# A mean in two parts and a product group in another place: a recurrent attention kernel with a SoLU layer

## The chip, the cores and the metric

The kernel runs on one core of a Trainium2 chip. The metric is the device time of one execution in microseconds (us), as the median of several runs. The core has five engines with their own instruction queues: TensorE (PE in the profile; its weight loads are PEld), VectorE (DVE), ScalarE (ACT), GpSimd (POOL) and SyncE (SP). Matrix products go to PSUM, and the other engines take them from there. DMAs are issued from the queues of SP, POOL and ACT.

## The reference

Two layers follow one another. The first is a recurrence over 768 steps for each of 4 x 8 heads with a state of 40 x 40. The second is a feed-forward layer with a softmax-weighted activation (SoLU) and a layer norm before the output product:

```python
for t in range(S):
    y[:, :, t] = np.einsum('bhd,bhde->bhe', rt, state)
    Sa = np.einsum('bhde,bhe->bhd', state, at)
    state_decay = state * wt[:, :, None, :] - np.einsum('bhd,bhe->bhde', Sa, bt)
    state = state_decay + np.einsum('bhd,bhe->bhde', vt, kt)
...
h = x @ w_in                                  # 3072 x 320 @ 320 x 1024
e = np.exp(h - np.max(h, axis=-1, keepdims=True))
solu = h * (e / (np.sum(e, axis=-1, keepdims=True) + 1e-09))
mu = np.mean(solu, axis=-1, keepdims=True)
var = np.mean((solu - mu) ** 2, axis=-1, keepdims=True)
return ((solu - mu) / np.sqrt(var + 1e-06) * g_ln) @ w_out
```

All inputs of the recurrence are float32. The weights `w_in` and `w_out` reach the kernel as 64-bit words, which it turns into float32 itself.

## The kernel before

The recurrence is done in chunks of 64 steps. Two of the four batches and all eight heads of one chunk make one unit of work, numbered `i` from 0 to 23. For each unit a triangular system is inverted, and the chunk's output and new state come out of products of 64 x 64 or 40 x 64 blocks, each of which uses a quarter of TensorE's array. The feed-forward layer takes the 128 finished rows of a unit some rounds later with products over the full array.

One main loop, `for i in range(-1, N + 3 + LAG)`, interleaves the stages of several units. A round `i` finishes unit `i`, prepares unit `i+1`, begins unit `j = i + 5`, and does the feed-forward layer for unit `m - 2 = i - 3` and its output for unit `m - 3 = i - 4`. The order of the instructions on PE, POOL, DVE and SP is the order in which the program text issues them; each of these engines works through its queue in that order. ScalarE's order is set by a planner. Synchronization follows from the tiles that instructions read and write, and from the buffers that tiles share.

The pieces that matter here, in the order of a round:

- `some(n)` issues n steps of the inversion (`prod` L404 and `uu` L406 on VectorE). `narrow` turns weights from 64-bit words to float32, on VectorE and ScalarE (L182 to L195), with some of those steps between. The eight chunks `c` of `w_out` (128 rows each) go to `w2[:, c]`; the sixth is turned at the end of round 2, the seventh and eighth in round 3.
- `carried` and `driven` (`px`), then `front(j)`: transposes of `a` and `b` of unit j (`pa`, `pb`); VectorE makes `aT` (L347) out of the first, ScalarE copies the second to `bT`. Then half of a feed-forward product, `hidden` (`h`).
- `solved` (`pu`), `attend_kv(i+1)` (transposes of k and v: `pk`, `pv`, copied by ScalarE to `kT`, `vT`), again `hidden`, `attend_rs(i+1)` (transposes of r and of the state: `pr`, `pst`), the rest of `hidden`, and `exped` (`nmax` L644 and `e` L647).
- `decay_turned` (`pei`, copied by ScalarE to `ex` L339), `scaled(j+1)` (two products on POOL, `kb` L318), `left(i-1)` (six DMAs on POOL, `xT<-x`).
- `answered` (`pl`, and VectorE's mask of it to `lu`), `norm(j)` (16 products `pnt` of bT and aT, VectorE's mask of them to `nt` L351, and a DMA of `nt` on POOL's queue L377), `flip` (`tu` L431), `weighed` and `spreadof`, `decay` (`pcum`).
- In round 4 (`i == 3 + LAG`) `centre_w2`: eight products `pmean` (L221) give the mean of the rows of `w2`, and one VectorE instruction (L222) subtracts it from all of `w2`. This takes the layer norm's mean out of the output product.
- `output(m-3, 0)` (`po` L692, first four of eight products with `w2`), `scores` (`ps`), `couple` (`py`), `output(m-3, 1)` (the rest of `po`, then `osb`), `close` (`pz`), `read` (`pyo`), `leave` (`x` L593), `folded` (`plnT`, copied to `lnT`). The first output is that of round 4.

A float32 product is issued as two passes, so the eight products of `pmean` are 16 instructions in the profile.

PSUM is divided among three pools: `banks` (two slots of two banks), `h` (one slot of two banks), and `bank` (two slots of one bank). `pa`, `pb`, `pk`, `pv`, `pr`, `pst`, `pei`, `pcum`, `pmean`, `po` and `plnT` share the two slots of `bank`; `px`, `pu`, `pl`, `pnt`, `ps`, `py`, `pz`, `pyo` share those of `banks`. A tile waits until the one that held its slot has been read.

Of the kernel before, what the change touches and what calls it, by code (L numbers as in the profile page):

```python
# [9 lines left out]
FP32 = mybir.dt.float32  # L10
# [4 lines left out]
ALU = mybir.AluOpType  # L15
PSUM = bass.MemoryType.PSUM
AX = mybir.AxisListType
P = 128
# [6 lines left out]
LAG = 1  # L25
# [23 lines left out]
def kernel(  # L49
# [18 lines left out]
    nc = tc.nc  # L68
    B, H, S, D = r.shape
    DM = H * D  # L70
# [4 lines left out]
    NF = DFF // P  # L75
# [5 lines left out]
    two = ctx.enter_context(tc.tile_pool(name="two", bufs=2))  # L81
# [14 lines left out]
    def c_(name):  # L96
        lo, hi = where[name]
        return cst[:, lo:hi]

    ident, tri = c_("ident"), c_("tri")  # L100
# [18 lines left out]
    for x in ex_t:  # L119
# [10 lines left out]
                          in_=c_("eye_hi").unsqueeze(1).to_broadcast([P, 8, Q]))  # L130
    w_in = const.tile([P, 2 * NK - 1, DFF // 2], FP32, name="w_in")
    w2 = const.tile([P, NF, DM], FP32, name="w2")
# [3 lines left out]
    def banks(name):  # L136
        return ps1.tile([P, 2, 512], FP32, tag="banks", name=name)

    def bank(name):
        return ps3.tile([P, 512], FP32, tag="bank", name=name)  # L140
# [74 lines left out]
        for x, y in zip(g_cols, (0, -20, -36)):  # L215
            nc.scalar.mul(out=x, in_=pg[:, 0:NF], mul=2.0 ** y)

    def centre_w2():
        t = bank("pmean")
        for c in range(NF):  # L220
            nc.tensor.matmul(t[:, 0:DM], lhsT=c_("mean"), rhs=w2[:, c, :], start=c == 0, stop=c == NF - 1)  # L221
        nc.vector.tensor_tensor(out=w2, in0=w2, in1=t[:, 0:DM].unsqueeze(1).to_broadcast([P, NF, DM]),  # L222
                                op=ALU.subtract)


    def half(p):
        return slice(C * p, C * p + C)
# [6 lines left out]
    def in_turn(tile_of, some=units):  # L234

        lots = {}
        for u in some:
            lots.setdefault(tile_of(*u), []).append(u)
        lots = list(lots.values())
        return [lot[n] for n in range(max(map(len, lots))) for lot in lots if n < len(lot)]  # L240

    def mm(o, lhsT, rhs, start=True, stop=True):
        nc.tensor.matmul(o, lhsT=lhsT, rhs=rhs, start=start, stop=stop, skip_group_check=True)  # L243
# [15 lines left out]
    def where_(i):  # L259
        return i % NPAIR, i // NPAIR  # L260

    def load(x, ap, i, queue=nc.sync):
        bp, ci = where_(i)
        for p in range(2):
            queue.dma_start(out=x[half(p), :, 0:D],  # L265
                              in_=ap[2 * bp + p, :, ci * C:(ci + 1) * C, :].rearrange("h t d -> t h d"))

    def ok(i):
        return 0 <= i < N


    def load_keys(i, names, queue=nc.sync):
        if not ok(i):
            return
        for n, ap in (("w", w), ("b", b), ("a", a), ("k", k)):
            if n in names:
                x = a_t[i % 4] if n == "a" else two.tile([P, H, D], FP32, tag="raw_" + n, name="raw_" + n,
                                                             bufs=3)
                st[i]["raw_" + n] = x
                load(x, ap, i, queue)  # L280
# [39 lines left out]
    def turned(name, x):  # L320
        t = bank("p" + name)
        for j in range(4):
            nc.tensor.transpose(out=t[0:W2, j * P:(j + 1) * P],  # L323
                                in_=x[:, 2 * j:2 * j + 2].rearrange("p a b -> p (a b)")[:, 0:W2], identity=ident)
        return t[0:W2].rearrange("p (j b t) -> p b j t", j=4, b=2)

    def tokens(name, bufs=1):
        return two.tile([P, 2, 4, C], FP32, tag=name, name=name, bufs=bufs)

    def kept(name, t, bufs=1):  # L330
        o = tokens(name, bufs)
        nc.scalar.copy(out=o[0:W2], in_=t)
        return o
# [16 lines left out]
    def masked(dst, t):  # L350
        nc.vector.tensor_tensor(out=dst, in0=t.rearrange("p b (j c) -> p b j c", j=4),  # L351
                                in1=tri.unsqueeze(1).unsqueeze(1).to_broadcast([P, 2, 4, C]), op=ALU.mult)

    def keyed(t, u):
        p, q, g, h = u
        return t[rows(h), p, 2 * q + g]
# [5 lines left out]
    def norm(i):  # L362
        if not ok(i):
            return
        d = st[i]
        t = banks("pnt")
        for u in in_turn(lambda p, q, g, h: (h, p ^ h)):
            p, q, g, h = u
            j = 2 * q + g
            mm(t[half(p ^ h), h, j * C:j * C + C], keyed(d["bT"], u), keyed(d["aT"], u))  # L370
        nt = d["nt"] = tokens("nt", AHEAD)
        masked(nt, t[:, :, 0:256])
        n, at = divmod(i, GRP)
        if at == 0:
            blocks[n] = dram.tile([2 * GRP * H, C, C], FP32, tag="nt_dram", name="nt_dram")
        queue = nc.sync if i < 4 else nc.gpsimd
        queue.dma_start(out=blocks[n].rearrange("(a h x) s c -> a x s h c", a=GRP, x=2)[at].rearrange("x s h c -> (x s) h c"),  # L377
                          in_=nt.rearrange("p h j c -> p (h j) c"))
# [36 lines left out]
    def bring(i):  # L415
        if not ok(i):
            return
        d = st[i]
        d["tu"], d["uh"] = tu_t[i % 2], uh_t[i % 2]
        n, at = divmod(i, GRP)  # L420
        src = inverse[n].rearrange("(e a h x) c t -> e a h x c t", e=2, a=GRP, x=2)
        for x in range(2):
            nc.sync.dma_start(out=d["tu"][C * x:C * x + Q, :, Q:2 * Q], in_=src[0, at, :, x].rearrange("h c t -> c h t"))
        for x in range(2):
            nc.sync.dma_start(out=d["uh"][C * x + Q:C * x + C], in_=src[1, at].rearrange("h x c t -> c (h x) t"))
# [40 lines left out]
    def attend_rs(i):  # L466
        if not ok(i):
            return
        d = st[i]
        bp, ci = where_(i)  # L470
        d["rT"] = kept("rT", turned("r", r_t[0]), 2)
        if ci:
            t = bank("pst")
            for x in range(4):
                nc.tensor.transpose(out=t[0:W2, x * P:(x + 1) * P],
                                    in_=st_t[bp][:, 2 * x:2 * x + 2].rearrange("p a b -> p (a b)")[:, 0:W2], identity=ident)
            d["s"] = two.tile([P, 4, P], FP32, tag="s", name="s")
            nc.scalar.copy(out=d["s"][0:W2], in_=t[0:W2].rearrange("p (x t) -> p x t", x=4))
# [148 lines left out]
    def hidden(i, some):  # L627

        if not ok(i):
            return  # L630
        d = st[i]
        for kt, x in some:
            if (kt, x) == (0, 0):
                d["h"] = ps2.tile([P, DFF], FP32, tag="h", name="h")
            part = slice(0, P) if kt < 2 else half(x)
            mm(d["h"][:, 512 * x:512 * x + 512], d["xT"][part, kt], w_in[part, 2 * kt + (x if kt < 2 else 0)],
               start=kt == 0, stop=kt == NK - 1)
# [64 lines left out]
    def some(n):  # L702
        while steps and n:
            if next(steps[0], steps) is steps:
                steps.pop(0)
            else:
                n -= 1
# [3 lines left out]
    def begin_inverse(n):  # L711
        steps.append(invert(n))
        next(steps[-1])
# [60 lines left out]
    for i in range(-1, N + 3 + LAG):  # L774
        j, m = i + AHEAD, i - LAG
        pieces = shares.get(i, (3, 6, 0, 6))
        some_weights = narrowed.get(i, (0, 0))

        some(pieces[0])
        if i >= 1:  # L780
            bring(i + 1)
        if i >= 0:
            load_values(i + 2)
        carried(i)
        driven(i)
        front(j)
        hidden(m - 2, ((0, 1),))
        load_keys(j + 3, "w")
        load_keys(j + 2, "bak")
        narrow(some_weights[0], pieces[1])  # L790

        solved(i)
        attend_kv(i + 1)
        hidden(m - 2, ((1, 1),))
        attend_rs(i + 1)
        hidden(m - 2, ((2, 0), (2, 1)))
        exped(m - 2)
        decay_turned(j + 1)
        scaled(j + 1)
        left(i - 1)  # L800

        answered(i)
        norm(j)
        if i >= 0:
            flip(i + 1)
        weighed(m - 2)
        spreadof(m - 2)
        decay(j + 2)
        if i == 0:
            turn_g()  # L810
        if i == 3 + LAG:
            centre_w2()
        output(m - 3, 0)
        if ok(j) and j % GRP == GRP - 1:
            begin_inverse(j // GRP)
        some(pieces[2])
        scores(i + 1)
        if i < 0:
            flip(i + 1)
        couple(i + 1)  # L820
        output(m - 3, 1)
        narrow(some_weights[1], pieces[3])

        close(i + 1)
        read(i, True)
        read(i, False)
        by_value(i + 2)
        leave(i)
        folded(m - 2)
        hidden(m - 1, ((0, 0), (1, 0)))  # L830
# [30 lines left out]
```

## Time and profile before

| | |
|---|---|
| median of 3 runs | 643.66 us (641.3 to 646.32) |
| the profiled execution: whole time | 642.36 us |
| its span | 640.3 us |
| mean granted clock of TensorE | 0.924 |
| PE busy | 565.3 us |
| DVE busy | 483.0 us |
| POOL busy | 269.1 us |
| ACT busy | 245.1 us |

A busy share is an average over stages with different limits. The span and the 2.1 us around it make the whole time of that one execution. Waits are read where they stand: "[3.00 <-DVE w L222]" behind an instruction says that its engine stood for 3.00 us and that the VectorE instruction of line 222, which writes `w`, ended it. In a line of the timeline the first number is the start in us from the begin of the span, the second the length in us; "x16" is the number of instructions that are merged in the line.

### The profile page before, as it was taken

How to read it: one execution, taken by the hardware profiler on the slowest of the kernel's cores; microseconds unless marked ns; L12 is line 12 of the kernel's file. 1: busy time of each engine (PE TensorE's matmuls, PEld its weight loads, DVE VectorE, ACT ScalarE, POOL GpSimd, SP SyncE). 2: the span in 40 equal slices, each digit the busy share in tenths (PEclk: the TensorE clock that was granted, in tenths of full speed). 3: DMA queues.
4: the chain of work that ended last, by engine and by line, in shares of the span. 5: the costliest groups of instructions: out<-in, count | busy, mean ns of one | idle time of the engine just before them, and what ended most of it. 6: DMA issues, size and time to landing. Idle time of an engine off the chain costs nothing.

```text
span 640.3 us, 26725 instructions
## 1 busy us (share of the span) xinstructions
PE 565.3 (88%) x11449; PEld 400.6 (63%) x11449; DVE 483.0 (75%) x1285; ACT 245.1 (38%) x497; POOL 269.1 (42%) x444
## 2 busy tenths in 40 slices
PE   4246597788889999999999999999999999999995
PEld 3124476656556767777667767776776676766653
DVE  4577798889858988878979889888887797433431
ACT  4313445553404334424433443443334333332221
POOL 3333355671524544472573545454624632322200
PEclk9665668797889999999999999999999999999998
DMA  8949896663426355454544554563523422210000
GB/s 165 161 76 161 166 170 129 136 138 70 89 53 112 79 112 111 85 111 92 111 98 96 108 101 99 108 124 74 109 52 70 101 45 50 51 37 26 24 20 20
DMA packets 217868, 59.92 MB, mean 94 GB/s; under 512 B 203216, under 2 KB 213048, under 8 KB 217752
## 3 DMA queue, kind: packets, MB, share of 16 engines
q1 hardware_dynamic: 200984, 34.47, 31.8%
q0 software_dynamic: 11376, 19.25, 12.5%
q10 hardware_dynamic: 5392, 4.51, 2.5%
q8 instruction: 90, 1.47, 1.0%
q14 instruction: 26, 0.21, 0.1%
HBM read 40.10 MB, written 13.37 MB: 84 GB/s over the span
## 4 chain that ended last, share of the span: by engine, by line
PE 70%; DVE 15%; DMA 7%; issue 3%; ACT 3%; SPq 1%; ACTq 0%; DVEq 0%; POOL 0%; POOLq 0%
PE po L692 16%; PE h L243 14%; PE pyo L243 7%; DVE prod L404 4%; PE pu L243 3%; PE px L243 3%; DVE uu L406 3%; PE ps L243 3%; DMA xT<-x 3%; PE plnT L681 2%; PE pl L243 2%; PE pz L243 2%; PE pei L323 2%; PE pk L323 2%; PE pr L323 2%
## 5 line engine op out<-in xcount | busy, mean ns | idle before, releaser
L404 DVE TENSOR_TENSOR prod<-blk,uu 128x30 f32<-128x30 f32 (+4 forms) x360 | 120.2, 334 | 16.4 <-DMA blk<-nt_dram 6.3
L243 PE MATMUL h<-w_in,xT 128*128 128x512 f32 (+1 forms) x288 | 122.0, 617 | 0.0
L692 PE MATMUL po<-w,lnT 128*128 128x320 f32 x384 | 115.2, 445 | 3.0 <-DVE w L222 3.0
L406 DVE TENSOR_TENSOR uu<-uu,prod 128x30 f32<-128x30 f32 (+4 forms) x360 | 105.7, 294 | 12.4
L692 PEld LDWEIGHTS po<-w,lnT 128*128 128x128 f32 x384 | 71.3, 192 | 33.2 <-issue 6.7
L644 DVE TENSOR_REDUCE nmax<-h 128x1 f32<-128x1024 f32 x24 | 29.4, 1224 | 56.4 <-PE h L243 56.4
L670 POOL TENSOR_TENSOR rs<-c,mhalf 128x1 f32<-128x1 f32 x24 | 13.4, 558 | 108.4 <-DVE c L669 108.4
L377 POOL DMA_DIRECT2D nt_dram<-nt x20 | 18.6, 929 | 89.1 <-DVE nt L351 76.3
L612 POOL TENSOR_TENSOR st<-tot,ex 104x160 f32<-104x160 f32 x44 | 22.2, 521 | 78.9 <-DVE tot L608 78.2
L243 PEld LDWEIGHTS h<-w_in,xT 128*128 128x128 f32 (+1 forms) x288 | 39.0, 191 | 21.7 <-issue 18.8
L624 POOL DMA_DIRECT2D xT<-x x96 | 48.7, 513 | 0.0
L682 ACT COPY lnT<-plnT 128x512 f32<-128x512 f32 x48 | 26.1, 588 | 43.6 <-PE plnT L681 39.9
L388 POOL DMA_DIRECT2D blk<-nt_dram x42 | 33.3, 798 | 18.0 <-DMA nt_dram<-nt 17.7
L243 PE MATMUL pyo<-lv,kb 64*64 64x104 f32 x768 | 37.9, 269 | 2.7
L647 ACT ACTIVATE e<-h,nmax 128x1024 f32<-128x1024 f32 x24 | 26.7, 1114 | 29.5 <-DVE nmax L644 28.5
L243 PE MATMUL pyo<-lu,kb 64*64 64x104 f32 x768 | 36.6, 262 | 0.0
L265 POOL DMA_DIRECT2D raw_r<-in_r_dram x48 | 35.0, 733 | 0.0
L653 DVE TENSOR_TENSOR e<-h,e 128x1024 f32<-128x1024 f32 x24 | 28.8, 1198 | 5.8 <-ACT e L647 5.8
L661 DVE BATCH_NORM_STATS2 bs<-e 128x6 f32<-128x512 f32 x48 | 30.9, 685 | 0.8
L443 ACT ACTIVATE wy<-py,cst 128x256 f32<-128x256 f32 x24 | 11.3, 472 | 52.4 <-PE py L243 52.4
L696 ACT ACTIVATE osb<-po,rs 128x320 f32<-128x320 f32 x24 | 12.7, 527 | 48.6 <-PE po L692 29.7
L318 POOL TENSOR_TENSOR kb<-raw_k,inv 128x320 f32<-128x320 f32 x24 | 21.6, 901 | 20.5 <-DMA raw_k<-in_k_dram 20.5
(125 smaller groups left out, 1133.8 us busy)
## 6 DMA issues: line engine op xcount, KB each, us to landing
blk<-nt_dram POOLq DMA_DIRECT2D x42, 128.0 KB, 3.7
nt_dram<-nt POOLq DMA_DIRECT2D x20, 256.0 KB, 4.0
raw_w<-in_w_dram SPq DMA_DIRECT2D x48, 80.0 KB
a<-in_a_dram SPq DMA_DIRECT2D x48, 80.0 KB
raw_r<-in_r_dram POOLq DMA_DIRECT2D x48, 80.0 KB, 3.3
lv<-in_v_dram SPq DMA_DIRECT2D x48, 80.0 KB
out_dram<-osb ACTq DMA_DIRECT2D x24, 160.0 KB
raw_b<-in_b_dram SPq DMA_DIRECT2D x44, 80.0 KB
```

The costliest lines, as they stand in the source:

```text
L243: nc.tensor.matmul(o, lhsT=lhsT, rhs=rhs, start=start, stop=stop, skip_group_check=True)
L265: queue.dma_start(out=x[half(p), :, 0:D], in_=ap[2 * bp + p, :, ci * C:(ci + 1) * C, :].rearrange("h t d -> t h d"))
L323: nc.tensor.transpose(out=t[0:W2, j * P:(j + 1) * P], in_=x[:, 2 * j:2 * j + 2].rearrange("p a b -> p (a b)")[:, 0:W2], identity=ident)
L388: queue.dma_start(out=nb[home:home + Q], in_=blocks[n][:, Q * e:Q * e + Q, Q * e:Q * e + Q])
L404: nc.vector.tensor_tensor(out=t, in0=nb[:, j:j + 1, j + 1:Q].to_broadcast([P, n_c, m]), in1=u[:, 0:n_c, j:j + 1].to_broadcast([P, n_c, m]) ...
L406: nc.vector.tensor_tensor(out=u[:, 0:n_c, j + 1:Q], in0=u[:, 0:n_c, j + 1:Q], in1=t, op=ALU.subtract)
L624: nc.gpsimd.dma_start(out=xT[to:to + Q, 2], in_=x[at + P - 3 * D:at + D, 2])
L644: nc.vector.tensor_reduce(out=nmax, in_=d["h"], axis=AX.X, op=ALU.max, negate=True)
L647: nc.scalar.activation(out=e, in_=d["h"], func=AF.Exp, bias=nmax, accum_out=d["esum"])
L653: nc.vector.tensor_tensor(out=d["e"], in0=d["h"], in1=d["e"], op=ALU.mult)
L661: nc.vector.bn_stats(out=bs[:, x], in_=d["e"][:, x * 512:x * 512 + 512])
L692: nc.tensor.matmul(d["out"][:, 0:DM], lhsT=d["lnT"][:, f, :], rhs=w2[:, f, :], start=f == 0, stop=f == NF - 1)
```

## The change

`centre_w2` is split in two functions. `mean_begun(6)` runs in round 3 (`i == 2 + LAG`), at the place in the round where `centre_w2` stood in round 4: it adds up the first six chunks in a `bank` slot and ScalarE copies the sum to an SBUF tile, which uses the buffer of `osb`. `centred(mean, 6)` runs in round 4 after the first `hidden` and ahead of `narrow` and `solved`: a product with the identity puts the sum back into a `bank` slot, two products add the last two chunks, and VectorE subtracts the mean from `w2` in two instructions of half the size. `norm(j)` moves in every round from behind `answered` to between `hidden(m-2, ((1, 1),))` and `attend_rs`.

```diff
-    def centre_w2():
+
+    def mean_begun(n):
         t = bank("pmean")
-        for c in range(NF):
-            nc.tensor.matmul(t[:, 0:DM], lhsT=c_("mean"), rhs=w2[:, c, :], start=c == 0, stop=c == NF - 1)
-        nc.vector.tensor_tensor(out=w2, in0=w2, in1=t[:, 0:DM].unsqueeze(1).to_broadcast([P, NF, DM]),
-                                op=ALU.subtract)
+        for c in range(n):
+            nc.tensor.matmul(t[:, 0:DM], lhsT=c_("mean"), rhs=w2[:, c, :], start=c == 0, stop=c == n - 1)
+        mean = two.tile([P, DM], FP32, tag="osb", name="mean", bufs=1)
+        nc.scalar.copy(out=mean, in_=t[:, 0:DM])
+        return mean
+
+    def centred(mean, n):
+        t = bank("pmean")
+        nc.tensor.matmul(t[:, 0:DM], lhsT=ident, rhs=mean, start=True, stop=False)
+        for c in range(n, NF):
+            nc.tensor.matmul(t[:, 0:DM], lhsT=c_("mean"), rhs=w2[:, c, :], start=False, stop=c == NF - 1)
+        for x in range(0, NF, NF // 2):
+            nc.vector.tensor_tensor(out=w2[:, x:x + NF // 2], in0=w2[:, x:x + NF // 2],
+                                    in1=t[:, 0:DM].unsqueeze(1).to_broadcast([P, NF // 2, DM]), op=ALU.subtract)
...
         driven(i)
         front(j)
         hidden(m - 2, ((0, 1),))
+        if i == 3 + LAG:
+            centred(mean, 6)
         load_keys(j + 3, "w")
...
         solved(i)
         attend_kv(i + 1)
         hidden(m - 2, ((1, 1),))
+        norm(j)
         attend_rs(i + 1)
...
         answered(i)
-        norm(j)
...
-        if i == 3 + LAG:
-            centre_w2()
+        if i == 2 + LAG:
+            mean = mean_begun(6)
         output(m - 3, 0)
```

## The prediction

> **What bounds the kernel now.** First the page's bars of 40 slices and the totals:
>
> ```profile
> PE 565.3 (88%) x11449; PEld 400.6 (63%) x11449; DVE 483.0 (75%) x1285; ACT 245.1 (38%) x497; POOL 269.1 (42%) x444
> ...
> PE   4246597788889999999999999999999999999995
> ...
> PEclk9665668797889999999999999999999999999998
> ```
>
> From the thirteenth slice on TensorE is at 9 and its clock is full; before that neither is. So there are two stages. The table of windows puts numbers on rounds of the main loop (`i`; a round starts with `px`):
>
> ```profile
> 217.40:239.60 22.20, 21.98 (x498) 15.69 (x493) 19.46 (x51) 9.23 (x19) 12.79 (x21) 1.00 0.55 110
> ...
> 171.00:181.20 10.20, 7.40 (x90) 4.76 (x86) 8.54 (x12) 2.70 (x6) 4.08 (x6) 1.00 0.41 88
> 181.20:184.60 3.40, 3.20 (x6) 2.19 (x7) 0.06 (x1) 0.00 (x0) 1.40 (x3) 0.50 0.32 86
> ```
>
> Columns: window, its length, then busy us of PE, PEld, DVE, ACT, POOL, granted clock, DMA share, GB/s. Round 6 (217.4) has PE busy 21.98 of 22.2 us; DVE has nearly 3 us to spare. From round 5 on, whatever PE must do more is paid in full. The other two windows lie in round 4, where the change works. Its timeline:
>
> ```profile
> 164.44 0.83 DVE L406 TENSOR_TENSOR uu<-uu,prod 128x126 f32<-128x126 f32 x1
> ...
> 165.81 0.68 DVE L347 TENSOR_TENSOR aT<-pa,ex 104x512 f32<-104x512 f32 x1
> ...
> 166.65 0.62 PE L323 MATMUL pv<-cst,v 128*104 128x128 f32 x4 [2.43 <-DVE aT L347]
> ...
> 173.93 4.47 PE L221 MATMUL pmean<-w,cst 128*128 128x320 f32 x16
> ...
> 178.44 2.82 DVE L222 TENSOR_TENSOR w<-w,pmean 128x2560 f32<-128x2560 f32 x1 [0.76 <-PE pmean L221]
> ...
> 181.40 3.98 PE L692 MATMUL po<-w,lnT 128*128 128x320 f32 x8 [3.00 <-DVE w L222]
> ...
> 185.32 0.69 PE L243 MATMUL ps<-aT,kT 40*64 40x64 f32 x32
> ```
>
> PE computes the mean (16 passes, 0.27 us apart), stands 3.00 us for the subtraction, and then runs `po` at half clock. `pv`, earlier, stood 2.43 us for `aT`: a wait on VectorE. For rounds 0 to 3, the waits between 60 and 195 us:
>
> ```profile
> PE pr L323 <- ACT kT L332: 6.0, 3, 2.2
> ...
> DVE lu L351 <- PE pl L243: 2.0, 2, 1.1
> ```
>
> PE waits about 2 us a round before `pr` (line: total, times, longest). The chain of waits runs through VectorE there (`prod`, `uu` and `w` steps), so a PE gap filled is worth only what VectorE gets from it: its two waits of about 1 us for `pl`.
>
> Last, a saturated round (10), for what the order of PE's groups costs:
>
> ```profile
> 308.06 1.02 PE L243 MATMUL h<-w_in,xT 128*128 128x512 f32 x2
> 309.01 0.69 PE L243 MATMUL pu<-tu,x 64*64 64x64 f32 x32
> ...
> 311.00 1.02 PE L243 MATMUL h<-w_in,xT 128*128 128x512 f32 x2
> 311.86 0.60 PE L323 MATMUL pr<-cst,r 128*104 128x128 f32 x4
> ...
> 314.46 0.69 PE L243 MATMUL pl<-rT,nuT 40*64 40x64 f32 x32
> 314.98 0.65 PE L243 MATMUL pnt<-aT,bT 40*64 40x64 f32 x32
> ```
>
> An `h` of two passes occupies 2 x 0.43 = 0.86 us. After the second one `pr` starts at once (311.86); after the first, the quarter-array `pu` starts 0.09 late (309.01 against 308.92). From the starts of single instructions likewise: quarter to full (`pu` to `pk`, `pnt` to `pcum`) 0.14, quarter to quarter (`pl` to `pnt`) 0.03.
>
> **The change, part by part, against the profiled execution (642.4 us whole, 640.3 its span).**
>
> *Mean out of round 4's end.* From pmean's start to `ps` is 11.39 us. What stays is eight `po` passes at full clock, 2.24 us (round 10: 316.20 to 318.44). That is -9.15. If the slow window stays, -7.5 (3.98 - 2.32 = 1.66 us less): the row first, `po` x8 took 3.98 here and 2.32 in round 10, in a window of clock 0.50 that follows the 3.00 us stall. [...]
>
> *First part, round 3.* Six chunks are 12 passes, 3.2 us, plus a ScalarE copy (`osb` from `po`, the same size, is 0.53). They stand between `pcum` (ends 145.9) and `ps`. Before, `ps` waits until 147.18 and `py` for `flip` until 148.19; `pyo` ends at 154.9, but VectorE takes it up only at 159.80 (`x`). So `ps` comes about 1.7 us later and 4.9 us cover it. Cost 0; +1.7 without that cover. ScalarE's `wy` queues behind the new copy, inside the same cover. `osb`'s buffer is not wanted until round 4's output.
>
> *Second part, round 4.* Identity and two chunks are 6 passes, 1.6 us, after `h` and before `pu`. They use up the 2.43 us stand for `aT`: cost 0, +1.6 without it. The subtraction (2 x 1.41 from 2.82) now stands on VectorE behind `aT` and ahead of the 12 inverse steps (3.5 us), `nt`, `nmax`, `lu`. Those start 2.8 later, where VectorE used to idle 1.78 us before `nmax` and 5.29 before `psi`. New is a third user of the two PSUM `bank` slots between `pb` and `pk`. The trace can't show which slot each takes. Low end: `pk` takes `pa`'s slot and `pv` follows `kT`'s copy, about 1.1 us after (`pk` 0.44, copy 0.59). High end: `pv` takes pmean's slot and waits for the whole subtraction, +2.9. Between them +2.0. No gain is possible in this item alone.
>
> *Norm earlier.* (a) Rounds 0 to 2: `pnt` (0.5 to 0.95 us) runs in the gap before `pr`, and `nt` (0.60) in VectorE's wait for `pl`. That is -0.4 in round 0 and -0.6 in round 1. In round 2 VectorE then meets ScalarE, which waits there for `raw_w` (`lw` at 128.35), so only -0.6 in all is counted. (b) POOL: `nt`'s one DMA (0.93 us to issue) now stands ahead of `kb`'s two products and `left`'s six DMAs, which therefore wait for `nt`. `kb` goes from 163.4 to about 170; its user `pb` comes a round later. `left` ends about 319.8 in round 10, with `x` rewritten at 325.3: 3 us of slack after a 2.2 us landing. The inverse's four loads on POOL stop waiting for `nt`'s landing (17.7 us in 4 waits), which lie under VectorE's work anyway: 0. SP's and ACT's queues are not passed by it. (c) `kb` leaves its place beside the inverse's steps. Row: `uu` took 0.83 beside `kb` at 164.44 and 0.28 elsewhere, `prod` just before 2.70 against 0.28; in round 3 two rows lost 0.94 together. [...] With 0.94 in round 3 the row gives -2.5. With (a) -3.1, of which PE's own chain, which reaches `pv` at about 164 to 166, allows part: I take -2.0, ends 0 and -3.0.
> (d) Saturated rounds 5 to 18, 14 of them: `pnt` between `h` and `pr` adds 0.09 + 0.14 and removes `pl` to `pnt` 0.03: +0.20 each, +2.8. Ends 0 and +5. No wait is there to win, since PE has none.
>
> Sum: -9.15 + 2.0 - 2.0 + 2.8 = -6.35, so 636.0. The median of the runs shown is 1.3 above the profiled execution: **637.3**.
>
> **Rivals.**
> *Full gain.* `pv` finds a slot at the low end and VectorE's advance carries whole: -9.15 + 1.1 - 3.0 + 2.8 = -8.3, and with fewer slow windows in round 3 (150.5 to 157.3 ran at 0.50) about -10: 633.7 to 635.4. For it: everything in round 4 up to `pv` follows VectorE. Against it: PE itself is needed for 1.6 us more before `pk`.
> *The wait comes back.* `pv` behind the subtraction, the six passes uncovered, the slow window kept, no advance: -7.5 + 2.9 + 1.6 + 2.8 = -0.2: 643.5. For it: `pv` waited on VectorE at just this place already.
> *Slower.* In each saturated round `po` takes the bank slot that ScalarE's `ex` copy frees. Now `ex` ends at 315.20 and `po` starts at 316.20; with `pnt` gone from between, the margin falls to about 0.5. Should ScalarE (whose order a planner sets) put the 1.11 us `e` ahead of `ex`, `e` waits for `nmax` (now ending near 316.0), `ex` ends near 317.7 and `po` waits 1.3 us: 14 x 1.3 = +18, less 6.35: about 655. It decides only if `e` precedes `ex`; in this trace `ex` goes first.
> That the first part isn't early is ruled out: its sixth chunk is ready at 135.2.
>
> **How the numbers follow.** Likeliest case 0.50 (634.5 to 640.5), full gain 0.22, wait back 0.16 (640.5 to 645), slower 0.12. From 632.5 to 643.5 leaves out the slower case and part of the third. One per cent, about what a measurement tells from no change, is 637.2: half of the first case and the second lie below it, faster 0.47; same 0.40; slower 0.13.
>
> **What would show it.** Right: `po` in round 4 without a wait and about 2.3 us long, `ps` there near 175 to 178, `pr` without its 2 us gaps in rounds 0 to 2, rounds of 22.4 us from 5 to 18. Wrong: a wait of `pv` or `pk` for `w` beyond 2.9 us, saturated rounds above 22.6, or a wait of `po` for `ex`.

## The result and the profile after

The changed kernel takes 640.24 us in the median of 9 runs (639.54 to 641.2), the kernel before 642.81 (640.72 to 647.47, 9 runs, those shown before among them). The ratio is 0.995, with a 95% interval from 0.9927 to 0.9973: about 3.2 us, a real gain of half a per cent. Forecast were 637.3 us and a ratio of 0.99. The profiled execution has a span of 637.7 us, against 640.3.

The bars of the page after, first TensorE and then its granted clock:

```profile
PE   5245677988999999999999999999999999999995
...
PEclk9665676688999999999999999999999999999998
```

The picture is the old one: a first stage in which TensorE is not full, and a saturated one. The clock is full from the eleventh slice to the last but one (1.00 from 159.3 to 633.7 us), and no slow slice follows in round 4.

Round 4 in the timeline (start, length, engine, line, operation; in brackets the idle time before it and what ended it):

```profile
163.19 0.43 DVE L415 TENSOR_TENSOR prod<-blk,uu 128x126 f32<-128x126 f32 x1
...
164.49 0.69 DVE L358 TENSOR_TENSOR aT<-pa,ex 104x512 f32<-104x512 f32 x1
165.58 0.70 PE L229 MATMUL pmean<-mean,cst 128*128 128x320 f32 x2
166.12 1.24 PE L231 MATMUL pmean<-w,cst 128*128 128x320 f32 x4
167.29 0.69 PE L254 MATMUL pu<-tu,x 64*64 64x64 f32 x32
...
167.39 2.89 DVE L233 TENSOR_TENSOR w<-w,pmean 128x1280 f32<-128x1280 f32 x2 [2.21 <-PE pmean L231]
...
170.43 0.62 PE L334 MATMUL pv<-cst,v 128*104 128x128 f32 x4 [1.42 <-DVE w L233]
...
176.38 2.32 PE L703 MATMUL po<-w,lnT 128*128 128x320 f32 x8
178.62 0.69 PE L254 MATMUL ps<-aT,kT 40*64 40x64 f32 x32
```

`po` no longer waits and runs at full clock. In its place two things are new, earlier in the round: `pu` waits until the six mean passes are through (165.58 to 167.29, 1.7 us), and `pv` waits 1.42 us for the second half of the subtraction. VectorE, which reached the subtraction early, stood 2.21 us for those passes.

Two saturated rounds in the table of windows (window, length, busy us of PE, PEld, DVE, ACT, POOL, clock, DMA share, GB/s), and TensorE inside one of them:

```profile
211.20:233.70 22.50, 22.28 (x488) 15.70 (x482) 16.56 (x47) 9.23 (x19) 12.83 (x21) 1.00 0.54 108
233.70:256.20 22.50, 22.28 (x486) 15.70 (x482) 18.28 (x54) 9.34 (x19) 9.21 (x17) 1.00 0.47 93
```

```profile
305.78 1.02 PE L254 MATMUL h<-w_in,xT 128*128 128x512 f32 x2
306.74 0.69 PE L254 MATMUL pnt<-aT,bT 40*64 40x64 f32 x32
307.36 0.64 PE L334 MATMUL pr<-cst,r 128*104 128x128 f32 x4
307.84 0.60 PE L486 MATMUL pst<-cst,st 128*104 128x128 f32 x4
```

The same products, but 22.5 us instead of 22.2. From `pr` to `pst` 0.48 us pass, where round 10 before had 0.44 (311.86 to 312.30).

In the first stage the work sits elsewhere. VectorE and POOL in round 1:

```profile
104.19 0.43 DVE L442 STREAM_TRANSPOSE tu<-tu 128x256 f32<-128x256 f32 x1
...
104.80 2.31 DVE L417 TENSOR_TENSOR uu<-uu,prod 128x96 f32<-128x96 f32 x1
107.14 0.26 DVE L415 TENSOR_TENSOR prod<-blk,uu 128x92 f32<-128x92 f32 x1
```

```profile
104.36 0.92 POOL L388 DMA_DIRECT2D nt_dram<-nt  x1 [0.55 <-DVE lu L362]
105.30 0.88 POOL L329 TENSOR_TENSOR kb<-raw_b,inv 128x320 f32<-128x320 f32 x1
106.12 0.86 POOL L329 TENSOR_TENSOR kb<-raw_k,inv 128x320 f32<-128x320 f32 x1
```

The same step of the inverse in round 1 before the change, and the longest one of round 4 before:

```profile
104.89 0.26 DVE L406 TENSOR_TENSOR uu<-uu,prod 128x96 f32<-128x96 f32 x1
...
161.70 2.70 DVE L404 TENSOR_TENSOR prod<-blk,uu 128x126 f32<-128x126 f32 x1
```

A step of the inverse that took 0.26 us before the change now takes 2.31. It ends at 107.11, 0.13 us after the second product of `kb`. In round 4 the long step of before is gone: `prod` at 163.19 takes 0.43 us, not 2.70.

VectorE leads the first stage, and so the start of `x` (first thing that it does with a round's result) is a good mark. From the timelines of the single executions:

```text
               x of    round to round (x to x)     x of     rounds 5 to 18
               round 0  0-1   1-2   2-3   3-4    round 4    (14 rounds, px to px)
before          94.2   20.7  20.4  24.6  32.4     192.2      309.0
after           94.9   21.8  20.9  23.6  24.2     185.5      313.1
e1 mean alone   93.8   21.7  20.2  25.2  26.5     187.5      309.4
e2 norm alone   94.7   21.9  20.9  23.2  30.0     190.6      313.1
e3 DMA late     92.9   20.7  19.9  25.6  26.8     185.9      313.1
e4 norm solved  95.8   21.4  20.4  24.5  24.2     186.3      309.7
e5 kb late      96.6   22.1  21.7  23.4  30.2     194.1      323.5
e6 mean banks   95.7   21.7  20.4  25.0  23.4     186.1      314.1
e8 one subtract 95.4   21.6  20.4  25.0  24.1     186.6      313.1
e9 all eight    95.2   21.4  20.4  24.4  27.2     188.5      313.2
```

The change wins 6.7 us up to round 4 and pays 4.1 us in the 14 saturated rounds. What follows them is equal. How far one execution can be trusted is seen in rows with the same code: after, e4, e6 and e8 don't differ before round 4, and yet the mark of round 0 spreads over 0.9 us, the steps 0-1 and 1-2 over 0.5 each, and the step 2-3 over 1.4. The step 3-4 of after and e4, which are the same there too, agrees within 0.1. So a difference counts below only where it is larger than that.

### The profile page after: what moved, and what is told of

The parts are those of the page before. It is cut to its first block, busy times and chain, and to the rows that moved or that the text cites. A ratio compares the mean times of both kernels' runs of the same rounds, so it can differ in the third digit from the quotient of the medians.

```text
span 637.7 us, 26729 instructions
## 1 busy us (share of the span) xinstructions
PE 567.5 (89%) x11451; PEld 399.6 (63%) x11451; DVE 461.9 (72%) x1286; ACT 245.3 (38%) x498; POOL 269.1 (42%) x444
## 4 chain that ended last, share of the span: by engine, by line
PE 71%; DVE 13%; DMA 6%; issue 4%; ACT 2%; SPq 2%; POOL 1%; DVEq 0%; ACTq 0%; POOLq 0%
PE h L254 16%; PE po L703 14%; PE pyo L254 7%; PE px L254 4%; PE pu L254 3%; DVE uu L417 3%; PE plnT L692 3%; PE ps L254 3%; DVE prod L415 3%; PE pl L254 2%; PE pr L334 2%; PE pnt L254 2%; PE pk L334 2%; PE pa L334 2%; PE pz L254 2%
## 5 line engine op out<-in xcount | busy, mean ns | idle before, releaser
L415 DVE TENSOR_TENSOR prod<-blk,uu 128x30 f32<-128x30 f32 (+4 forms) x360 | 99.0, 275 | 24.0 <-DMA blk<-nt_dram 14.0
L703 PE MATMUL po<-w,lnT 128*128 128x320 f32 x384 | 113.5, 440 | 0.0
L417 DVE TENSOR_TENSOR uu<-uu,prod 128x30 f32<-128x30 f32 (+4 forms) x360 | 101.9, 283 | 12.4
L664 DVE TENSOR_TENSOR e<-h,e 128x1024 f32<-128x1024 f32 x24 | 29.4, 1225 | 10.1 <-ACT e L658 10.1
L254 PEld LDWEIGHTS pnt<-aT,bT 40*64 40x64 f32 x768 | 14.6, 144 | 26.5 <-issue 25.0
L254 PEld LDWEIGHTS pyo<-lv,kb 64*64 64x64 f32 x768 | 23.9, 145 | 11.3 <-issue 7.7
```

Of the source, the lines that this page charges most:

```text
L415: nc.vector.tensor_tensor(out=t, in0=nb[:, j:j + 1, j + 1:Q].to_broadcast([P, n_c, m]), in1=u[:, 0:n_c, j:j + 1].to_broadcast([P, n_c, m]) ...
L417: nc.vector.tensor_tensor(out=u[:, 0:n_c, j + 1:Q], in0=u[:, 0:n_c, j + 1:Q], in1=t, op=ALU.subtract)
L664: nc.vector.tensor_tensor(out=d["e"], in0=d["h"], in1=d["e"], op=ALU.mult)
L703: nc.tensor.matmul(d["out"][:, 0:DM], lhsT=d["lnT"][:, f, :], rhs=w2[:, f, :], start=f == 0, stop=f == NF - 1)
```

## The experiments

All were timed against the kernel before on the same chip; each ratio is that of the runs, with its 95% interval.

**e1, e2: each part alone.** e1 is the changed kernel with norm put back; e2 is the kernel before with norm moved.

```diff
 e1
         hidden(m - 2, ((1, 1),))
-        norm(j)
         attend_rs(i + 1)
...
         answered(i)
+        norm(j)
```

> Only the mean's part of the change; norm stays behind answered. Theory A (the mean wins about 10 us in round 4, and norm's move loses it again: 3.8 us in rounds 0 to 2 by POOL's kb products falling on inverse steps, and 4.1 us in rounds 5 to 18 by array switches): rounds 5 to 18 at 22.2 us as before, round 4 begins near 159 us and lasts about 26, and the time is about 633 us, ratio 0.985. Rival B (both parts of the change give a little, the mean's gain being eaten by the wait of pv): about 640, ratio 0.995. Rival C (pyo's wait for lv, a PSUM slot given in another order, is what costs in rounds 0 to 3, and comes from the extra bank tile): pyo still waits, round 4 begins near 163, about 637.

> The kernel before with only norm(j) moved. Theory A: round 4 begins near 163 us, rounds 5 to 18 take 22.5 us, the time is 4 + 4 = 8 us above before, about 651, ratio 1.012. Rival B: at or under before, ratio 0.995 to 1.0. Rival C: pyo does not wait for lv, only the saturated rounds lose, +4 us, ratio 1.006.

Measured: e1 637.95 us, ratio 0.9909 (0.9879 to 0.9938); e2 644.84, ratio 1.0009 (0.9987 to 1.0031). So the whole gain comes from the mean, about 5.9 us. Norm's move alone makes no difference that its interval shows; on top of the mean it costs about 0.4% (0.995 against 0.991, with intervals that just overlap). But theory A, as it was put, had both sizes too large. In the table norm alone is 4.1 us dearer in the saturated rounds, as expected, but up to round 4 it is 1.6 us *ahead* of before, not 4 behind. Of its steps only one differs by more than the scatter: from round 3 to 4 it wins 2.4 us, as the changed kernel does over e1 (2.3). The loss of 1.2 us in step 0-1 is not clear of it: e1, without norm's move, has nearly the same step. The mean alone wins 4.7 us up to round 4. TensorE's waits in e1's first stage name two waits that this part brings (engine, what waited, for what: us in total, times, longest):

```profile
PE pv L334 <- DVE w L233: 1.4, 1, 1.4
...
PE pmean L229 <- DVE aT L358: 1.1, 1, 1.1
```

The second of them says that the passes don't fill the stand for `aT`: `pmean` waits for `aT` itself. Rival C falls as well: e2 has no extra bank tile, and `pyo` waits for `lv` there too (4.8 us in 3 waits). Nor does that wait set a round's length: round 1 has 2.5 us of it in e4 and takes 21.4 us, none in e6 and takes 21.7.

**e3: norm early, its DMA at the old place on POOL**, so that POOL's order is that of before.

```diff
     def norm(i):
...
         masked(nt, t[:, :, 0:256])
+        if i < 4:
+            norm_sent(i)
+
+    def norm_sent(i):
...
         answered(i)
+        norm_sent(j)
```

> The changed kernel, with the DMA of nt issued on POOL at its old place behind answered, so that POOL's order is that of before (kb, left, then nt's DMA), while the products and VectorE's mask stay early. Theory A: no inverse step behind flip lasts over 1 us in rounds 0 to 2, round 4 begins at 158 to 159.5 us, the saturated rounds stay at 22.5, the time is about 636, ratio 0.989. Rival C (PSUM slot order): pyo still waits for lv and nothing changes, about 640, ratio 0.995.

Measured: 640.86 us, ratio 0.9966 (0.9946 to 0.9985): no difference from the changed kernel (0.995), against theory A's 0.989. Yet the profile did most of what the theory says in rounds 0 to 2: no step behind `flip` lasts over 1.24 us, and the mark of round 2 lies at 133.5 us, against 137.5 to 137.7 in after, e4, e6 and e8. How much of that is gained is not sharp: e7 and e10, further down, have e3's code in these rounds and reach the mark at 136.0. Between the marks of 2 and 4 all of it is lost again (52.4 us, against 47.8 to 49.1 in those four). The timeline of round 4 in e3 shows how:

```profile
161.05 2.71 DVE L422 TENSOR_TENSOR prod<-blk,uu 128x126 f32<-128x126 f32 x1
163.79 0.83 DVE L424 TENSOR_TENSOR uu<-uu,prod 128x126 f32<-128x126 f32 x1
```

```profile
161.28 1.43 POOL L276 DMA_DIRECT2D raw_r<-in_r_dram  x2
162.72 0.88 POOL L329 TENSOR_TENSOR kb<-raw_b,inv 128x320 f32<-128x320 f32 x1
163.54 0.92 POOL L329 TENSOR_TENSOR kb<-raw_k,inv 128x320 f32<-128x320 f32 x1
```

The two long steps of before are back, with `kb` behind the two DMAs. POOL's order thus sets *which* steps of the inverse stand still: with `kb` ahead of `nt`'s DMA those before `aT` in rounds 3 and 4, with `kb` behind it those after `flip` in rounds 0 to 2. What the one order wins in one place, the other wins in the other.

**e4: norm directly behind solved from round 5 on.**

```diff
         solved(i)
+        if i >= 5:
+            norm(j)
         attend_kv(i + 1)
         hidden(m - 2, ((1, 1),))
-        norm(j)
+        if i < 5:
+            norm(j)
```

> The changed kernel, but in rounds 5 and later norm(j) stands directly behind solved, quarter-array products behind quarter-array products. If the 0.29 us a saturated round come from TensorE's switches between full and quarter array, they vanish: 22.2 us a round, 4 us less than the changed kernel, about 636, ratio 0.989. If they come from something that norm holds up by being early (kT, rT, the bank slots), they stay or grow, since norm is earlier still; a wait of pnt for aT would show as rounds above 22.6.

Measured: 636.17 us, ratio 0.988 (0.9852 to 0.9907), 4 us under the changed kernel (4.5 by the two ratios), as expected. Window and timeline of e4:

```profile
211.00:233.20 22.20, 21.98 (x483) 15.69 (x482) 17.01 (x48) 9.34 (x19) 12.83 (x21) 1.00 0.53 108
```

```profile
304.11 0.67 PE L254 MATMUL pnt<-aT,bT 40*64 40x64 f32 x32
304.72 0.65 PE L334 MATMUL pk<-cst,kb 128*104 128x128 f32 x4
305.20 0.60 PE L334 MATMUL pv<-cst,v 128*104 128x128 f32 x4
305.64 1.02 PE L254 MATMUL h<-w_in,xT 128*128 128x512 f32 x2
306.50 0.60 PE L334 MATMUL pr<-cst,r 128*104 128x128 f32 x4
```

`pnt` follows `pu` (quarter behind quarter), `pr` follows `h` at once (305.64 + 0.86 = 306.50), and the round is back at 22.2 us. So the 0.29 us a round are the switches between quarter and full array, and `aT` is ready in time even there.

**e5: POOL's order alone.** The kernel before, norm where it was, `kb` and `left` behind it.

```diff
-        scaled(j + 1)
-        left(i - 1)
-
         answered(i)
         norm(j)
+        scaled(j + 1)
+        left(i - 1)
```

> The kernel before with one thing changed: on POOL kb's products and left's DMAs are issued behind norm's DMA, norm itself stays behind answered. Theory A (what norm's move does in rounds 0 to 4 is POOL's order: kb leaves the inverse steps ahead of aT and falls on those behind flip): steps of 1 to 2.3 us behind flip in rounds 0 to 2, none of 2.7 us ahead of aT in rounds 3 and 4, from the x of round 0 to that of round 4 about 1.5 to 3 us shorter in sum, saturated rounds still 22.2, the time about 642, ratio 0.997. Rival (the early gain is TensorE's filled gap before pr): nothing gained, only the new collisions, ratio 1.002 to 1.004.

Measured: 657.58 us, ratio 1.0192 (1.0155 to 1.023). Neither expectation holds as a whole. One part of theory A does: in round 4 no step ahead of `aT` is long, and from round 3 to 4 e5 takes 30.2 us, nearly what e2 takes (30.0) and 2.2 less than before. The step that took 2.70 us before, in e5:

```profile
165.73 0.43 DVE L404 TENSOR_TENSOR prod<-blk,uu 128x126 f32<-128x126 f32 x1
```

But the rounds ahead of that lose more, so that e5's mark of round 4 is 194.1, against 192.2 before; the rest, 14.5 us, is lost in rounds 5 to 18 (323.5 us). TensorE's and then VectorE's waits between 217 and 500 us:

```profile
PE pv L323 <- DVE prod L404: 10.1, 6, 1.8
```

```profile
DVE uu L398 <- DMA blk<-nt_dram: 19.7, 6, 3.4
```

With norm at its old place `kb` and six DMAs come so late on POOL that the loads of the next inverse, which are issued behind them, are late by up to 3.4 us in every second round. VectorE is then late with `aT`, and `pv`, whose PSUM slot it frees, stands. The moved norm has the same order on POOL without this, as its `nt` begins 3.1 us earlier in a saturated round (7.0 us after `px` at 300.53 in the changed kernel, 10.1 us after it before). So the order on POOL that the change brings is affordable only together with the early norm. In round 4, e5 and e3 say the same from two sides: POOL's order alone wins what e2 wins there (2.2 of 2.4 us), and taking that order back loses it again.

**e6: the second mean tile in another PSUM pool**, so that `pv`'s slot isn't its own.

```diff
     def centred(mean, n):
-        t = bank("pmean")
-        nc.tensor.matmul(t[:, 0:DM], lhsT=ident, rhs=mean, start=True, stop=False)
+        t = banks("pmean")
+        nc.tensor.matmul(t[:, 0, 0:DM], lhsT=ident, rhs=mean, start=True, stop=False)
...
```

> The changed kernel with the second mean tile in a slot of the pool banks in place of bank. Theory A (pv waits 1.4 us for the second half of the subtraction only because its bank slot is the mean's): pv waits no more for w in round 4, 1.5 us less than the changed kernel, about 638.8, ratio 0.9925. Rival (VectorE's work is the bound there, the wait moves to pnt, pr or nmax): as the changed kernel, ratio 0.995.

Measured: 640.45 us, ratio 0.993 (0.9907 to 0.9953). The wait of `pv` for `w` is gone, and the step from the mark of round 3 to that of round 4 is 0.8 us shorter than after (23.4 against 24.2). But in round 5 `pv` waits in its place, by the waits between 185 and 215 us:

```profile
PE pv L334 <- DVE prod L415: 0.6, 1, 0.6
```

VectorE still has the 2.8 us of subtraction and what stood behind it to work off. Round 5 takes 23.3 us from `px` to `px`, where the changed kernel takes 22.5: the 0.8 us are given back. The wait moved, and the times can't be told apart: the rival was right in this. So `pv`'s slot isn't what bounds round 4; VectorE's work is.

**e8: one subtraction instead of two halves.**

```diff
-        for x in range(0, NF, NF // 2):
-            nc.vector.tensor_tensor(out=w2[:, x:x + NF // 2], in0=w2[:, x:x + NF // 2],
-                                    in1=t[:, 0:DM].unsqueeze(1).to_broadcast([P, NF // 2, DM]), op=ALU.subtract)
+        nc.vector.tensor_tensor(out=w2, in0=w2, in1=t[:, 0:DM].unsqueeze(1).to_broadcast([P, NF, DM]),
+                                op=ALU.subtract)
```

> The changed kernel with the mean taken out of w_out in one VectorE instruction in place of two halves. Theory A (the first user of the result, po, comes 6 us later, and pv's slot is free only after all of it): no difference, ratio 0.995, pv waits 1.4 us as before. Rival (the halves let something start early): 1 us more or over.

Measured: 640.92 us, ratio 0.9939 (0.9917 to 0.9961), `pv` waits 1.4 us for `w` as in the changed kernel. The halves are worth nothing here.

**e9: no first part; all eight products in round 4's new place.**

```diff
-        nc.tensor.matmul(t[:, 0:DM], lhsT=ident, rhs=mean, start=True, stop=False)
...
-            centred(mean, 6)
+            centred(None, 0)
...
-        if i == 2 + LAG:
-            mean = mean_begun(6)
```

> The changed kernel without the first part of the mean: all eight products (16 passes) stand in round 4 between the first h and pu, and no product with the identity. Theory A (whatever TensorE does there is paid in full, because pu, pk and the subtraction all queue behind it; the part done in round 3 is hidden): 10 passes more at that place, 2.7 us more than the changed kernel, less about 0.5 in round 3, so about 642.3, ratio 0.998; VectorE's wait for pmean grows from 2.2 to about 4.9 us. Rival (the split into two parts is worth nothing, moving the subtraction away from po is all): as the changed kernel, ratio 0.995.

Measured: 642.55 us, ratio 0.9967 (0.9947 to 0.9987). The intervals of this and of the changed kernel overlap, so the profile has to decide:

```profile
165.79 4.55 PE L230 MATMUL pmean<-w,cst 128*128 128x320 f32 x16
170.28 0.69 PE L253 MATMUL pu<-tu,x 64*64 64x64 f32 x32
...
173.41 0.62 PE L333 MATMUL pv<-cst,v 128*104 128x128 f32 x4 [1.42 <-DVE w L232]
```

16 passes take 4.49 us from the first to `pu`, instead of 1.71 for six. Everything behind is later by as much, and `pv`'s wait of 1.42 us is unchanged. From the mark of round 3 to that of round 4 e9 takes 27.2 us, 3.0 more than the changed kernel; VectorE waits 5.0 us for `pmean` instead of 2.2. So the ten passes more are not covered by anything at that place.

**e7, e10: what the runs favour, in one kernel.** e7 joins e4; e3's order on POOL up to round 2 and the changed kernel's from round 3 on; e6's PSUM slot; and seven chunks in the mean's first part. e10 is e7 with norm behind solved only from round 7 on.

```diff
 e7
+        if not 4 <= i < AHEAD + 3:
+            norm_sent(i)
...
+        if i < 3:
+            norm_sent(j)
...
-            centred(mean, 6)
+            centred(mean, 7)
...
-            mean = mean_begun(6)
+            mean = mean_begun(7)
```

> All that the runs so far favour in one kernel: norm by solved from round 5 on; nt's DMA at its old place on POOL up to round 2 and ahead of kb from round 3 on; seven chunks in the first part of the mean, one in the second; the second mean tile in banks. Theory A: 4.1 (switches) + about 4 (collisions of rounds 0 to 2) + 0.5 (one chunk of TensorE's work moved into round 3) + 1.5 (pv's wait) less than the changed kernel: about 630, ratio 0.979. If the gains in rounds 0 to 2 only bring VectorE earlier to another wait: 634, ratio 0.985.

> The combined kernel with norm by solved only from round 7 on, norm between the transposes in rounds 5 and 6. Theory A (in round 5 VectorE is still behind after the subtraction, and pnt by solved waited 1.15 us for aT): that wait goes, two rounds pay 0.29 us for the switches, about 0.6 us less than the combined kernel, ratio 0.984. Rival (the lag of VectorE shows up as another wait in round 5): no difference, ratio 0.985.

Measured: e7 635.11 us, ratio 0.9848 (0.982 to 0.9875); e10 635.72, ratio 0.9878 (0.9848 to 0.9908). e7 beats both the kernel before and the changed one, but the four gains don't add up to theory A's 630: it is the second of its two expectations. Against e4 (0.988) the mending of rounds 0 to 4 gives a fraction of a per cent, inside the intervals. In round 5 VectorE's lag shows, in e7 as the first and in e10 as the second of these waits (184 to 260 us):

```profile
PE pnt L254 <- DVE prod L422: 0.9, 1, 0.9
```

```profile
PE pv L334 <- DVE prod L422: 1.0, 1, 1.0
```

Putting norm elsewhere there only gave the wait another name, as e10's rival had it. Round 5 takes 23.4 us in e7 and 23.7 in e10, but 22.2 in e4, which leaves the mean's tile in `bank`: e6's slot moved the wait here too.

## Why the prediction was right, and which of its terms were not

The direction was right, and so was what bounds each stage. The sum was -6.35; the measured ratio makes -3.2 us, so only half of the forecast gain came. The prediction had put 0.47 on a gain of over one per cent and 0.40 on a change of less than that; less came. The time lies in its likeliest case (634.5 to 640.5), but only 0.3 us from its end. By its terms:

- **Mean out of round 4's end, -9.15: as predicted.** After, eight `po` passes take 2.24 us from their start to `ps` (176.38 to 178.62), without a wait and at full clock. 11.39 - 2.24 = 9.15 is gone from this place. The prediction's other value, -7.5, was for a slow window that stays. It did not stay: 181.20 to 184.60 ran at 0.50 before, and without the stall of 3.00 us the clock of round 4 is 1.00 from 162.4 to 188.1. The last section shows behind which windows half clock came.
- **First part in round 3, 0: nothing against it.** From the mark of round 2 to that of round 3 e1 is 0.6 us over before, and the changed kernel 0.4 over e2. Both are inside the scatter of that step (1.4 us), so they may be nothing.
- **Second part in round 4, +2.0: mis-sized, +3.3.** The prediction had the six passes "use up the 2.43 us stand for `aT`: cost 0", and took only a part of the subtraction for `pv`'s wait. In the changed kernel the passes cost their 1.71 us and `pv` then 1.42 more, with about 0.16 until its start: 3.3. The stand was no cover. In e1, where `aT` is late as before, `pmean` waits for `aT` (1.1 us), so the passes come behind the stand and not into it; and the subtraction can only begin after the passes. Where norm is moved too, `aT` comes earlier and the stand isn't there at all. Lengthening the passes (e9) moves everything by the full amount. With norm's move and without it the sum is the same: in step 3-4 the mean wins 5.9 us in e1 over before, and 5.8 in the changed kernel over e2, which is 9.15 less 3.3. The prediction's range for `pv` (a slot at the low or the high end) was not what mattered: with another slot (e6) the 0.8 us that round 4 wins go in round 5.
- **Norm early, -2.0: about right in sum (-1.6 in e2), wrong in its parts; that the sum fits is luck.** The gaps before `pr` did not close: TensorE still waits 4.5 us for `kT` there in three waits (6.0 before), although the prediction's sign of being right was that they go. The prediction saw `kb` leave the steps before `aT`, but not where it would land: on the steps behind `flip`, in rounds 0 to 2. 2.31 us for one step in round 1 is that. On the other side more was won in round 4 than the 1.55 us that are in the prediction's -2.5 for it: 0.55 of `uu`, by its row, and 1.0 of `prod`, an estimate from the time that it ran on behind the two DMAs (163.35 to 164.40), which no run shows. In place of the 1.0 the runs showed 2.27: `prod` fell from 2.70 to 0.43 us, and `uu` from 0.83 to 0.29, although the two DMAs of `raw_r` still stand beside them (163.42 to 164.86). That `kb`'s place decides is shown by e3, where `kb` and the 2.71 us came back, and by e5. How is not: by the trace `prod` had stood for 1.67 us, beside the end of `st` and two DMAs, when `kb` began (161.70 and 163.37 before).
- **Saturated rounds, +2.8: mis-sized, +4.1.** The starts of groups gave 0.20 us a round; 0.29 were paid. The gaps between groups grew by 0.21; the rest is that a group's own start is slower behind a switch (`pr` to `pst` 0.48 instead of 0.44, and the 32 `pnt` passes, from the first start to the last, 0.48 instead of 0.43). e4 removed the switches and with them all of it.

Of the rivals, "the wait comes back" described best what happened to the mean: `pv` waited on VectorE as said, only without the slow window. The slower case, `po` behind `ex`, did not come: no TensorE wait is shown from 217 to 460 us.

With the measured terms: -9.15 + 0.5 + 3.3 - 1.6 + 4.1 = -2.9, against -2.6 between the two spans. The terms that are off all err to the same side, by 3.5 us together; 2.6 of that are the second part and the saturated rounds.

## What to carry to other kernels

A wait that the profile shows is a place to hide work only for work that isn't on the way to what ends the wait, or to what would end it next: ask what the moved work's result holds up, and whether another part of the same change removes the wait. On an engine without a gap, order costs too: keep products that use the array alike together (e4 made 0.7% of that). When one instruction moves on an in-order queue, follow everything that it displaces to where it lands, and ask what runs beside it there.

## What the runs showed of the hardware

- Steps of the inverse on VectorE took longer in places where GpSimd's products `kb` (128x320) ran beside them. `uu` (128x126) took 0.83 us at 164.44 before, with `kb` from 163.37 to 165.12, and 0.29 at 163.65 in the changed kernel, without it. `uu` (128x96) took 2.31 us in round 1 of the changed kernel, beside both products, and 0.26 before. `kb` itself took 0.86 to 0.93 us in these places. The longest steps began before `kb` did: by 0.50 us in round 1 of the changed kernel, while GpSimd issued a DMA, and by 1.67 in round 4 before. Beside two such DMAs without `kb` behind them `uu` took 0.29 us (163.65 in the changed kernel). `nmax` took 1.23 us beside `kb` at 309.58 in the changed kernel, and 1.23 at 314.03 before, with GpSimd idle. In the changed kernel:

```profile
309.42 0.87 POOL L329 TENSOR_TENSOR kb<-raw_b,inv 128x320 f32<-128x320 f32 x1
309.58 1.23 DVE L655 TENSOR_REDUCE nmax<-h 128x1 f32<-128x1024 f32 x1 [1.39 <-PE h L254]
```

- In the traces before and after, the granted clock is 1.00 or 0.50 and changes after whole multiples of 3.41 us. The first row is the window before `po` in round 4 before the change, with most of the 3.00 us stall in it, and the next window had half clock. The second is the window in the changed kernel into which most of `pv`'s 1.42 us falls; the next was full, and so were all up to 633 us.

```profile
177.80:181.21 3.41, 0.60 (x3) 0.09 (x1) 2.77 (x1) 0.00 (x0) 3.12 (x5) 1.00 0.25 72
...
169.52:172.93 3.41, 2.50 (x42) 1.71 (x43) 3.12 (x10) 0.96 (x2) 0.00 (x0) 1.00 0.65 112
```

In these two traces 228 such windows with full clock lie between 20 and 500 us. All 13 with TensorE busy for less than 2.0 us were followed by one at half clock, and none with more than 2.4 us was. Between these both happened before the change: 2.07 us busy from 126.60 on was followed by full clock, 2.38 from 147.08 on by half.

- The order of a few instructions on POOL's queue moved the whole kernel by 2% (e5, ratio 1.0192), though its edit changes nothing but their order: between 217 and 500 us VectorE waited 19.7 us for loads queued behind them, in 6 waits of up to 3.4 us.
